# Attention scores of every pass as float32 products in quarters of the array

## The chip, the core and the metric

The kernel runs on one core of a Trainium2 chip. TensorE (PE in the profile) multiplies matrices, VectorE (DVE), ScalarE (ACT) and GpSimd (POOL) do the rest, and SyncE (SP) issues the DMAs, one after another. The metric is the device time of one execution in microseconds; less is better.

## What is computed

Eight batches of eight heads of block-causal attention (576 positions, head size 64, blocks of 64), and behind it a feed-forward layer with a squared ReLU:

```python
scores = scale * np.matmul(q, k.transpose(0, 1, 3, 2))
mask = block_i >= block_j
scores = np.where(mask, scores, -1000000000.0)
scores = scores - np.max(scores, axis=-1, keepdims=True)
attn = np.exp(scores)
attn = attn / (np.sum(attn, axis=-1, keepdims=True) + 1e-09)
out = np.matmul(attn, v)
x = out.transpose(0, 2, 1, 3).reshape(B * S, H * D)      # 4608 x 512
h = x @ w_in                                             # 512 x 2048
g = np.maximum(h, 0.0) ** 2
return g @ w_out                                         # 2048 x 512
```

All arrays are float32. The result is wanted to about float32 precision, so the kernel splits most operands into a high and a low fp16 part and adds two or three fp16 products.

## The kernel before

**Passes.** The attention is cut into 40 passes. A pass takes two heads of one batch (head 0 on partitions 0 to 63, head 1 on 64 to 127) and some of the nine query tiles of 64 rows; query tile j sees key blocks 0 to j. Passes 0 to 7 (batches 0 and 1) take tiles 0 to 2, passes 8 to 15 tiles 3 to 8 of the same batches, and passes 16 to 39 (six batches, four pairs of heads) all nine tiles. The tables G_210, G_86 and so on say which tiles share one score tile `ps` of 1024 columns (two PSUM banks of 512), and at which column each begins. A pass of nine tiles has 45 blocks of 64 queries by 64 keys for each head, in three groups.

**One group** (`softmax`, L431) is a chain: `scores` (L404) on PE into `ps`; row maxima on DVE (L446); exponentials on ACT (L452); the reciprocal of the sums on DVE (L461); the weights into `p_rows`, high part on ACT (L475), low part on DVE (L476); then a transposing DMA into `p_turned` (L480). `values` (L512) multiplies v with `p_turned` into `px`, one accumulation for tiles 0 to 2 and one for tiles 3 to 8. The first 12 passes keep the weights in float32 and turn them on PE (L507) instead.

**Scores, two ways.** Passes 0 to 15 are "native" (NATIVE = 16): q of each head stands alone in a tile `qz` with zeros in the other head's 64 partitions, and a float32 product over all 128 rows of the array writes the head's 64 columns (L411). Passes 16 to 39 use fp16 parts: `front` (L352) takes the largest |q| and |k| (L363), scales, and writes high and low parts into `qs`, `k1` and `k2` (ACT L382, L383; DVE L384, L387, L390, L391); three transposing DMAs (L394 to L396) bring them to `qT` and `kT` with the high part of a head on 64 partitions and its low part on the other 64. Each block of scores is then two fp16 products over 128 rows (z = 0 and 1, L422). In both ways the two heads use the two column halves of the array at once. `front` also makes the fp16 parts of v (L364, L399, L400).

**Loads.** `load(passes[i+2])` stands at the end of pass i. Native passes load `qz` and `kf`, the others `qk32` (tag "qk32", three buffers), and all load v (L347, L349). The same three "qk32" buffers serve the 32 loads of w_out rows: `wa` for the scale, `wb` for the parts (L203 to L206), during passes 8 to 15.

**The feed-forward layer** works on 12 chunks of 384 tokens. `moe_in` (L661) has 16 hidden slices `ph` of 12 fp16 products (L670), then ACT, POOL and DVE form g; `moe_out` (L685) has three outputs `po` of 48 products (L695). These products are laid between the steps of the passes: `pour` takes a set number of them per pass (FILL), `defer` puts `values` and `normalize` a number of such steps later. Before that the weights are split: `weight_parts` (L273) needs DVE, ACT and POOL for each of 16 slices of w_in and 16 of w_out. `first_moe` (chunk 0) has the w_out slices made while it runs.

**Order.** A scheduler with a model of time sets the order of each engine's instructions once, when the program is built; on the chip every engine takes its own in that order. SP, too, issues its DMAs strictly in order, and one that waits holds up those behind it.

## Time and profile before

Three runs took 1155.17 us (median), 1152.74 to 1156.35 us. The profiled execution is one more:

| | |
|---|---|
| profiled execution, own time | 1157.18 us |
| its span, first to last instruction | 1155.4 us |
| mean granted TensorE clock | 0.963 |
| PE busy | 1035.3 us (90%) |
| DVE busy | 763.9 us (66%) |
| ACT busy | 629.6 us (54%) |
| POOL busy | 341.0 us (30%) |
| DMA engines busy, hardware queue | 55.2% |

A row of a group of instructions reads: line, engine, operation, output<-input, shapes, count | busy us, mean ns of one | idle time of the engine before them and what ended it. In a row of the windows each engine has its busy time and, in brackets, its instructions; then come the granted clock (1.00 is full), the share of time in which the DMA engines were busy, and GB/s. A matmul's duration contains its way through the array, so matmuls overlap; the time that one takes from the next is seen in the starts.

### The profile page before, as it was taken

What the parts mean: (1) busy time and instruction counts of PE and PEld (TensorE: products, weight loads), DVE (VectorE), ACT (ScalarE), POOL (GpSimd) and SP (SyncE); (2) the same over time, 40 slices, a digit from 0 to 9 for tenths busy, and PEclk for the clock granted to TensorE, in tenths of its full rate; (3) what the DMA queues carried; (4) which work ended last, traced back from release to release, by engine and by line L of the source; (5) the groups of instructions that cost most, each with busy time, mean ns of one, the idle gap of its engine ahead of it and who ended that gap; (6) DMA issues with size and microseconds to landing.
All of it is one profiled execution on the core that took longest, in us unless ns stands there. A gap on an engine that the chain in (4) does not pass through costs nothing. (4 is left out here: it accounts for less than half of the span.)

```text
span 1155.4 us, 18711 instructions
## 1 busy us (share of the span) xinstructions
PE 1035.3 (90%) x6836; PEld 541.6 (47%) x6836; DVE 763.9 (66%) x1783; ACT 629.6 (54%) x1492; POOL 341.0 (30%) x312
## 2 busy tenths in 40 slices
PE   6679777898989989899997999889889999999998
PEld 4234322354445445445544545445445545555453
DVE  6998789869778978868749857976896613212120
ACT  6586765557468548726737627726865723223140
POOL 2575145124112412422205302520340314312030
PEclk9799998899999999999999999989999999999999
DMA  8555177867687688855954657567848330000000
GB/s 282 194 186 194 56 193 188 198 140 140 144 165 156 114 191 164 155 115 114 186 120 84 141 111 138 119 140 148 170 80 169 48 78 20 10 19 1 28 1 28
DMA packets 337948, 142.25 MB, mean 123 GB/s; under 512 B 309696, under 2 KB 323008, under 8 KB 337856
## 3 DMA queue, kind: packets, MB, share of 16 engines
q1 hardware_dynamic: 337856, 141.06, 55.2%
q8 instruction: 53, 0.87, 0.3%
q14 instruction: 39, 0.32, 0.1%
HBM read 55.31 MB, written 9.44 MB: 56 GB/s over the span
## 5 line engine op out<-in xcount | busy, mean ns | idle before, releaser
L670 PE MATMUL ph<-xt,w1h 128*128 128x384 f16 x1536 | 381.2, 330 | 21.7 <-ACT r L676 10.4
L695 PE MATMUL po<-w2h,g 128*128 128x512 f16 x1152 | 359.7, 386 | 8.5 <-ACT w2h L291 8.5
L679 POOL TENSOR_TENSOR r<-r 128x384 f32<-128x384 f32 x192 | 178.6, 936 | 556.4 <-ACT g L678 520.3
L695 PEld LDWEIGHTS <-g 128*128 128x128 f16 x1728 | 166.3, 99 | 219.4 <-issue 34.1
L670 PE MATMUL ph<-xt,w1l 128*128 128x384 f16 x768 | 253.3, 330 | 0.0
L695 PE MATMUL po<-w2l,g 128*128 128x512 f16 x576 | 222.1, 386 | 4.2 <-POOL w2l L292 4.2
L670 PEld LDWEIGHTS <-w1h 128*128 128x128 f16 x1536 | 145.0, 99 | 129.6 <-issue 34.4
L452 ACT ACTIVATE p<-ps,nmx,es 128x320 f32<-128x320 f32 (+8 forms) x216 | 131.1, 616 | 135.9 <-DVE nmx L449 111.4
L676 ACT ACTIVATE r<-ph 128x384 f32<-128x384 f32 x192 | 93.2, 491 | 160.3 <-PE ph L670 147.9
L680 DVE TENSOR_TENSOR g<-r,g 128x384 f16<-128x384 f32 x184 | 113.7, 623 | 86.3 <-POOL r L679 86.2
L476 DVE SCALAR_TENSOR_TENSOR p_rows<-p,rs,p_rows 128x320 f16<-128x320 f32 (+8 forms) x240 | 143.5, 632 | 18.6 <-ACT p_rows L475 18.3
L475 ACT ACTIVATE p_rows<-p,rs 128x320 f16<-128x320 f32 (+8 forms) x240 | 120.3, 569 | 47.1 <-DVE rs L461 23.1
L446 DVE TENSOR_REDUCE nmx<-ps 128x1 f32<-128x192 f32 (+8 forms) x288 | 124.6, 479 | 23.5 <-PE ps L422 14.8
L678 ACT ACTIVATE g<-r 128x384 f16<-128x384 f32 x192 | 99.4, 525 | 4.0 <-POOL w1l L292 0.8
L670 PEld LDWEIGHTS <-w1l 128*128 128x128 f16 x768 | 75.8, 99 | 51.2 <-issue 2.2
L422 PE MATMUL ps<-kT,qT 128*64 128x64 f16 (+6 forms) x960 | 84.7, 297 | 10.6 <-DMA qT<-qs 5.8
L534 PE MATMUL px<-p_turned,v 128*64 128x384 f16 (+5 forms) x1168 | 79.3, 282 | 14.5 <-DMA p_turned<-p_rows 10.1
L702 DVE TENSOR_SCALAR ob<-po,uv 128x512 f32<-128x512 f32 x36 | 28.9, 805 | 95.7 <-PE po L695 95.7
L534 PEld LDWEIGHTS <-v 128*64 128x64 f16 x1128 | 54.7, 115 | 48.1 <-issue 22.1
L604 POOL TENSOR_TENSOR x<-x,hb 128x768 f32<-128x768 f32 (+1 forms) x16 | 44.6, 2785 | 94.9 <-DVE hb L595 92.8
L422 PEld LDWEIGHTS <-qT 128*64 128x64 f16 x960 | 45.9, 111 | 50.5 <-issue 31.7
L606 POOL TENSOR_TENSOR xt<-x,xt 128x768 f16<-128x768 f32 (+1 forms) x16 | 51.7, 3229 | 30.9 <-DVE xt L605 24.3
(129 smaller groups left out, 965.3 us busy)
## 6 DMA issues: line engine op xcount, KB each, us to landing
qk<-in_qk SPq DMA_DIRECT2D x24, 576.0 KB, 4.5
wa<-in_w_out SPq DMA_DIRECT2D x16, 512.0 KB, 4.3
wb<-in_w_out SPq DMA_DIRECT2D x16, 512.0 KB, 4.4
out<-ob SPq DMA_DIRECT2D x32, 256.0 KB, 2.1
vraw<-in_vm SPq DMA_DIRECT2D x30, 256.0 KB, 3.5
w1raw<-in_w_in SPq DMA_DIRECT2D x8, 512.0 KB, 6.6
kf<-in_qkt SPq DMA_DIRECT2D x8, 288.0 KB, 3.6
w2h<-in_w_in SPq DMA_DIRECT2D x4, 512.0 KB, 10.9
```

The costliest lines, as they stand in the source:

```text
L422: nc.tensor.matmul(ps[hs, o].rearrange("p (n d) -> p n d", d=D), t["qT"][:, j, hs], t["kT"][:, z, c0:c1, hs], start=(z == 0), stop=(z == 1),)
L446: nc.vector.tensor_reduce(nmx[:, i : i + 1], ps[:, off : off + w], axis=AX.X, op=ALU.max, negate=True)
L452: nc.scalar.activation(p32[:, off : off + w], ps[:, off : off + w], AF.Exp, bias=nmx[:, i : i + 1], scale=es, accum_out=sm[:, i : i + 1],)
L475: nc.scalar.activation(hi, p32[:, off : off + w], AF.Copy, scale=rs[:, i : i + 1])
L476: nc.vector.scalar_tensor_tensor(lo, p32[:, off : off + w], rs[:, i : i + 1], hi, op0=ALU.mult, op1=ALU.subtract)
L534: nc.tensor.matmul(px[hs, D * a :].rearrange("p (j d) -> p j d", d=D), lhs, rhs, start=(c == 0 and pi == 0), stop=(c == NCH[g] - 1 and (pi ...
L670: nc.tensor.matmul(ph[:, :CH], w[:, f, P * cc : P * cc + P], xt[:, z, cc, :], start=(i == 0), stop=(i == 11))
L676: nc.scalar.activation(r, ph[:, :CH], AF.Relu, scale=c)
L678: nc.scalar.activation(g[:, 0], r, AF.Square)
L679: nc.gpsimd.tensor_tensor(r, r, r, op=ALU.mult)
L680: (nc.gpsimd if f < G_POOL and ck < G_CK else nc.vector).tensor_tensor(g[:, 1], r, g[:, 0], op=ALU.subtract)
L695: nc.tensor.matmul(po, gs[f][:, z, P * t : P * t + P], w[:, f, :], start=(i == 0), stop=(i == 3 * NF - 1))
```

## The change

All 40 passes get their scores from float32 products, with no fp16 parts of q and k. q and k of a pass are loaded as they are (`qk32`: head h on its 64 partitions), and a product uses only the 64 rows of its head and 64 columns: a quarter of the array. Even query tiles write the columns of their own head, odd query tiles the columns of the other head, so four products can be in four different quarters. The tables are laid out anew so that even tiles lie in the first bank of `ps` and odd tiles in the second. Where an even tile reaches into the second bank (the last block of tile 8, and tile 0 beside it), the product uses all 128 rows with a zero-padded q (`qzs`, two constant tiles, loaded by two small DMAs per pass). `behind` fixes the order of the products of one group among themselves: odd head 0, odd head 1, even head 0, even head 1.

Since odd tiles now hold the heads in swapped halves, `values` has to pick the columns of `p_turned` from alternating halves. `picked` does so: two neighbouring tiles in one product, a left-over tile in one of its own.

```diff
-NATIVE = 16
...
+G_4321 = [(4, 0), (2, 320), (3, 512), (1, 768)]
+G_850 = [(8, 0), (5, 576), (0, 960)]
+G_85 = [(8, 0), (5, 576)]
+G_76 = [(7, 512), (6, 0)]
 G_43 = [(4, 0), (3, 512)]
-G_75 = [(7, 0), (5, 512)]
-G_86 = [(8, 0), (6, 576)]
-G_210 = [(2, 0), (1, 192), (0, 320)]
-G_4230 = [(4, 0), (2, 320), (3, 512), (0, 768)]
-G_751 = [(7, 0), (5, 512), (1, 896)]
+G_210 = [(2, 0), (1, 512), (0, 192)]
...
-G_Y = [(G_86, [], []), (G_75, [3], []), (G_43, [0], [1])]
-G_XY = [(G_4230, [], []), (G_751, [0], [0]), (G_86, [3], [1])]
+G_Y = [(G_85, [], []), (G_76, [3], []), (G_43, [0], [1])]
+G_XY = [(G_4321, [], []), (G_850, [0], [0]), (G_76, [3], [1])]
...
+    qzs = [const.tile([P, 2, 2, D], F32, name=f"qz{i}") for i in range(2)]
+    for t in qzs:
+        for h in range(2):
+            nc.gpsimd.memset(t[D - D * h : P - D * h, h], 0.0)
...
-        for h in range(2):
-            hs, zs = slice(D * h, D * h + D), slice(D - D * h, P - D * h)
-            nc.gpsimd.memset(t[zs, :, h], 0.0)
-            nc.sync.dma_start(t[hs, :, h], qkt[b, hps, hs, 0, :T3].rearrange("c p s -> p c s"))
-        nc.sync.dma_start(t[:, :, 2], qkt[b, hps, :, 1, :T3].rearrange("c p s -> p c s"))
+        for c in range(2):
+            nc.sync.dma_start(t[:, c], qkt[b, hp + c, :, :, :T3])
...
-        if t["native"]:
...
-            t["raw"] = p2.tile([P, 2, S], F32, tag="qk32", name=f"qk32_{u}", bufs=3)
-            nc.sync.dma_start(t["raw"], qk[b - 1, hp])
+        t["qk"] = p2.tile([P, 2, S], F32, tag="qk32", name=f"qk32_{u}", bufs=3)
+        nc.sync.dma_start(t["qk"], qkt[b, hp])
+        t["qz"] = qzs[i % 2]
+        for h in range(2):
+            hs = slice(D * h, D * h + D)
+            nc.sync.dma_start(t["qz"][hs, h], qkt[b, hp, hs, 0].rearrange("p (j d) -> p j d", d=D)[:, 0:9:8, :])
...
-            nc.vector.tensor_reduce(st[:, 0:2], raw, axis=AX.X, op=ALU.max, apply_absolute_value=True)
...
-            nc.scalar.activation(k1[:, :, 0:D], k3, AF.Copy, scale=s[:, 1:2])
-            nc.scalar.activation(qs[:, :, 0:D], q3, AF.Copy, scale=s[:, 0:1])
...
-            nc.vector.tensor_copy(k2[:, :, D:P], k1[:, :, 0:D])
-            nc.vector.tensor_copy(k2[:, :, 0:D], k1[:, :, D:P])
...
-            nc.sync.dma_start_transpose(kT[:, 0], k1.rearrange("p j d -> p (j d)"))
-            nc.sync.dma_start_transpose(qT, qs.rearrange("p j d -> p (j d)"))
-            nc.sync.dma_start_transpose(kT[:, 1], k2.rearrange("p j d -> p (j d)"))
...
+    def scores(t, ps, group):
+        parts = ([], [])
+        for j, off in group:
+            c0 = 0
+            while c0 <= j:
+                c1 = min(j + 1, c0 + 8 - (off // D + c0) % 8)
+                parts[j % 2].append((off + D * c0, j, c0, c1))
+                c0 = c1
+        parts[0].sort()
+        last = None
+        for i in range(max(map(len, parts))):
+            for p in (1, 0):
+                if i >= len(parts[p]):
+                    continue
+                o, j, c0, c1 = parts[p][i]
                 for h in range(2):
+                    hs, rs = slice(D * h, D * h + D), slice(D * (h ^ p), D * (h ^ p) + D)
+                    if o >= 512 and not p:
+                        q, k = t["qz"][:, h, j // 8], t["qk"][:, 1, D * c0 : D * c1]
+                    else:
+                        q, k = t["qk"][hs, 0, D * j : D * j + D], t["qk"][hs, 1, D * c0 : D * c1]
+                    mm = nc.tensor.matmul(ps[rs, o : o + D * (c1 - c0)], q, k, start=True, stop=True)
+                    if last is not None:
+                        behind(mm, last)
+                    last = mm
...
+    def picked(turned, o, n, a, g, h, px):
+        t, e = a, turned.shape[1] + a
+        while t < e:
+            m = (e - t) // 2
+            side = h ^ ((t + 3 * g) & 1)
+            if m:
+                st = n + 1 - 2 * side
+                v = turned[:, t - a : t - a + 2 * m].rearrange("p (m t) b d -> p m (t b) d", t=2)
+                rhs = v[:, :, o + side : o + side + st + 1 : st, :]
+                yield px[:, D * t : D * (t + 2 * m)].rearrange("p (m t d) -> p m t d", t=2, d=D), rhs
+            else:
+                m = 0.5
+                yield px[:, D * t : D * t + D], turned[:, t - a, o + side]
+            t += int(2 * m)
...
+                if not whole and g and c == 2:
+                    a = 0
...
-                native=i < NATIVE, whole=i < WHOLE, last=hp == NHP - 1,
+                whole=i < WHOLE, last=hp == NHP - 1,
```

The host side only arranges the input `qkt` for all eight batches and drops `qk`. Nothing is changed in the feed-forward layer, in FILL and DELAY, or in the softmax but for the scale of the exponential, which is now a constant in all passes.

**The order on PE, first group of pass 24 (batch 4, heads 0 and 1).** `ps` are its scores, `ph` the products of `moe_in` of chunk 4. Before, every block comes as two pairs of fp16 products (each row stands four times):

```order
L670 MATMUL ph_4_6_4949<-xt_4_4141,w1l_97 128x384
L422 LDWEIGHTS qT_4_0_0_4776
L422 MATMUL ps_4_0_0_4_5010<-kT_4_0_0_4777,qT_4_0_0_4776 64x320
...
L422 MATMUL ps_4_0_0_4_5010<-kT_4_0_0_4777,qT_4_0_0_4776 64x192
...
L422 MATMUL ps_4_0_0_4_5010<-kT_4_0_0_4777,qT_4_0_0_4776 64x256
...
L422 MATMUL ps_4_0_0_4_5010<-kT_4_0_0_4777,qT_4_0_0_4776 64x64
L183 LDWEIGHTS ones_bf_78
```

The same group now; where the dots stand, there are the twelve products of a slice `ph`:

```order
L657 MATMUL ph_4_6_4764<-xt_4_4019,w1l_103 128x384
L389 MATMUL ps_4_0_0_4_4827<-qk32_4_0_0_4482 64x256 x2
L657 LDWEIGHTS w1h_102
L657 MATMUL ph_4_7_4789<-xt_4_4019,w1h_102 128x384
...
L389 MATMUL ps_4_0_0_4_4827<-qk32_4_0_0_4482 64x320 x2
L389 MATMUL ps_4_0_0_4_4827<-qk32_4_0_0_4482 64x128 x2
L389 MATMUL ps_4_0_0_4_4827<-qk32_4_0_0_4482 64x192
L657 LDWEIGHTS w1h_102
L657 MATMUL ph_4_8_4808<-xt_4_4019,w1h_102 128x384
...
L389 MATMUL ps_4_0_0_4_4827<-qk32_4_0_0_4482 64x192
```

The group, whole before, now stands in three pieces: the odd tile 3 (256 columns) is alone, and the second head of tile 2 (192) comes twelve products behind the first. Over the 72 groups of passes 16 to 39 there were 118 pieces and 36 unbroken groups before; now there are 111 pieces and 44 unbroken groups, as the one of pass 18, where the rows 64x256, 64x320, 64x128 and 64x192 follow each other.

**The order on SP, the loads of passes 12 and 13 and of w_out.** `qz`, `kf` and `qk32` 1_0 and 1_1 are the q and k of passes 12 and 13, `wb1` the slices of w_out, `vraw` v. Before:

```order
L205 DMA wb1_0_1399<-in_w_out 128x512
L205 DMA wb1_1_1408<-in_w_out 128x512
...
L205 DMA wb1_2_1417<-in_w_out 128x512
L334 DMA qz_1_0_3_1387<-in_qkt 64x384 x2
L335 DMA kf_1_0_3_1388<-in_qkt 128x576
...
L334 DMA qz_1_1_3_1647<-in_qkt 64x384 x2
L335 DMA kf_1_1_3_1648<-in_qkt 128x576
...
L205 DMA wb1_3_1473<-in_w_out 128x512
```

Now:

```order
L327 DMA qk32_1_0_3_1393<-in_qkt 128x1152
L340 DMA vraw1_81<-in_vm 128x2x256
L210 DMA wb1_0_1402<-in_w_out 128x512
...
L210 DMA wb1_1_1411<-in_w_out 128x512
L331 DMA qz0_89<-in_qkt 64x2x64 x2
L210 DMA wb1_2_1420<-in_w_out 128x512
...
L210 DMA wb1_13_1645<-in_w_out 128x512
L342 DMA vraw0_80<-in_vt 64x2x64
L327 DMA qk32_1_1_3_1654<-in_qkt 128x1152
L210 DMA wb1_14_1660<-in_w_out 128x512
```

The q and k of pass 13 moved from before `wb1_3` to behind `wb1_13`, since they now take turns with w_out in the three "qk32" buffers. On PE the scores of pass 13 moved with them: from before the first product of `moe_out` of chunk 0 to behind 78 of its 144.

More of the change, by code (lines that the diff above doesn't have):

```diff
@@ L316, in load_first @@
             passes[NHP * b + hp + c].update(
-                qz=[t[:, c, h] for h in range(2)], kf=t[:, c, 2], chunks=2, v32=o, es=D**-0.5
+                qk=t[:, c], chunks=2, v32=o, es=D**-0.5
             )
@@ L441, in softmax @@
         rs = small.tile([P, n], F32, tag="rs", name=f"rs_{gu}")
-        for j, off in group:
-            scores(t, ps, j, off)
+        scores(t, ps, group)
         for i, (j, off) in enumerate(group):
@@ new lines, in values @@
+                runs = [picked(blocks, o, n, a, g, h, px[D * h : D * h + D]) for h in range(2)]
+                for k, pair in enumerate(zip(*runs)):
+                    for h, (dst, rhs) in enumerate(pair):
+                        nc.tensor.matmul(
+                            dst,
+                            t["v32"][:, h, c, :] if whole else t["v16"][:, zv, h, c, :],
+                            rhs,
+                            start=(c == 0 and pi == 0 and k == 0),
+                            stop=(c == NCH[g] - 1 and (pi == 2 or whole)),
+                            skip_group_check=True,
+                        )
@@ L544, in attention_moe_kernel @@
+        nc.scalar.activation(x, px, AF.Copy, scale=2.0**-A_P if whole else t["xsc"])
     xts = {}
```

117 lines of the change are left out of this document (24 added, 93 removed).

## The prediction

> **What bounds the kernel now.** I read the six stages in the windows first (columns: PE, its weight loads, DVE, ACT, POOL, granted clock, DMA share, GB/s).
>
> ```profile
> 0.00:50.00 50.00, 29.68 (x229) 18.88 (x230) 36.30 (x123) 29.59 (x94) 18.34 (x36) 0.80 0.85 275
> 50.00:100.00 50.00, 38.07 (x239) 20.43 (x239) 49.96 (x98) 37.40 (x82) 37.07 (x34) 1.00 0.51 169
> 100.00:140.00 40.00, 35.73 (x225) 18.32 (x221) 27.82 (x80) 30.06 (x74) 9.95 (x17) 1.00 0.34 103
> 140.00:215.00 75.00, 52.70 (x248) 20.06 (x248) 67.19 (x139) 41.12 (x82) 34.00 (x24) 0.82 0.71 184
> 215.00:910.00 695.00, 639.58 (x4560) 338.02 (x4559) 530.30 (x1252) 426.40 (x1038) 178.85 (x139) 0.97 0.70 139
> 910.00:1155.00 245.00, 239.56 (x1340) 125.87 (x1339) 52.30 (x96) 65.06 (x128) 62.77 (x63) 1.00 0.08 22
> ```
>
> The last 245 us are feed-forward products almost without a gap; so whatever PE finishes earlier up to 910 moves the end by as much. From 215 to 910, the passes with fp16 scores, PE is the bound with 55.4 us of idle time (695 - 639.6) and a clock of 0.97, that is some 21 us of lost clock. From 50 to 100 DVE is the bound (49.96 of 50), from 140 to 215 nearly (67.2 of 75): there PE waits for the weights' parts. Then the waits of PE from 215 to 910 (us in total, times, longest):
>
> ```profile
> PE px L534 <- DMA p_turned<-p_rows: 9.2, 6, 2.5
> PE ph L670 <- DVE ob L702: 7.0, 5, 3.1
> PE ph L670 <- ACT r L676: 6.9, 10, 2.1
> PE nq L589 <- DVE sq L584: 6.5, 4, 2.8
> PE ps L422 <- DMA qT<-qs: 5.8, 4, 3.6
> PE pm L183 <- DVE dg L182: 3.4, 3, 2.0
> PE ps L422 <- ACT p L452: 3.4, 3, 1.5
> PE iv L621 <- DVE ivs L624: 3.0, 2, 2.1
> PE ps L422 <- DMA kT<-k: 1.3, 2, 1.1
> ```
>
> No single wait rules; DVE ends most of them. The lost clock goes with the gaps, as two stretches of 25 us show:
>
> ```profile
> 325.00:350.00 25.00, 21.90 (x182) 12.74 (x181) 20.28 (x47) 18.93 (x46) 6.44 (x6) 0.93 0.78 166
> 575.00:600.00 25.00, 25.00 (x155) 11.82 (x155) 10.36 (x28) 9.84 (x25) 0.00 (x0) 1.00 0.70 140
> ```
>
> With 3.1 us of idle PE the clock is 0.93 on the mean, without any it is full. So a gap costs more than its length.
>
> **The change part by part: the scores on PE.** What a block of 64 by 64 costs both heads is read from starts in the timeline of PE (start, duration, group):
>
> ```profile
> 411.13 0.38 PE L695 MATMUL po<-w2l,g 128*128 128x512 f16 x1
> 411.35 0.38 PE L695 MATMUL po<-w2h,g 128*128 128x512 f16 x1
> 411.66 0.95 PE L422 MATMUL ps<-kT,qT 128*64 128x512 f16 x8
> 412.44 0.48 PE L534 MATMUL px<-p_turned,v 128*64 128x192 f16 x10
> ...
> 22.77 0.88 PE L411 MATMUL ps<-first 128*64 128x192 f32 x12
> 23.48 0.61 PE L534 MATMUL px<-p_turned,vraw 128*64 128x192 f32 x8
> ```
>
> The eight fp16 products are 512 and 384 score columns, two products each, for both heads: 0.78 us until the next group starts, for 14 blocks, 0.056 us a block. The twelve float32 products are two groups of 192, 128 and 64 columns: 0.71 us for 12 blocks, 0.059 us. The column halves work side by side: a `po` product of 512 columns starts 0.22 us before the next, 0.42 ns a column, so the four products of 896 columns would need 1.5 us one after another and took 0.78. So a float32 product costs what two fp16 products cost, as long as only column halves overlap. All that can be won is that now the two row halves work at once as well. No product of before does that. If they don't, nothing is won; if they do fully, only the longer parity counts: 8 blocks in the first group of a pass, 8 and the two zero-padded ones in the second, 8 in the third, 26 in place of 45. But the order breaks groups up. I walked through the 72 groups of passes 16 to 39 as they stand in it, every product starting no earlier than the one before and than its quarter is free, and every piece by itself: 769 block lengths instead of 24 x 26 = 624, and 1173 if the row halves took turns. In time: 24 x 45 x 0.056 = 60.5 us before; now between 769 x 0.059 = 45.4 and 1173 x 0.059 = 69.2 us. I take the lower end, since the column halves do overlap fully in these rows: -15, with +9 as the other bound. The Trainium skill, "TensorE: Matmul & The Clock Gate", Part 3, measures four strips of 32 rows at 3.07 times one strip; by that share, an estimate from its figure, about a quarter of the 24 us between the ends would be missing and the sum 6 us longer. No run here shows it.
>
> Each change of the shape in which the array is used costs a start: 411.35 to 411.66 is 0.31 us where the product alone takes 0.22. Counted through PE's order there are 505 such changes instead of 454: 51 x 0.09 = +5, between 0 and +10.
>
> **The values.** For the short price I take two rows of a window of one `values` (417 to 419.2 us):
>
> ```profile
> L534 PE MATMUL px<-p_turned,v 128*64 128x384 f16 x12 | 1.2, 330 | 0.0
> L534 PE MATMUL px<-p_turned,v 128*64 128x64 f16 x6 | 0.3, 195 | 0.0
> ```
>
> A column costs (330 - 195)/320 = 0.42 ns. In the third key chunk a sixth tile is multiplied: three pairs of 64 columns in 28 passes, 28 x 3 x 0.027 = 2.3 us. The left-over tiles make 228 more pairs with no column more; I give them under 1 us in all, at most 0.03 us each. Together +3, at most +9.
>
> **DVE, ACT and SP.** These groups go, all off PE's path:
>
> ```profile
> L363 DVE TENSOR_REDUCE st<-qk 128x2 f32<-128x1152 f32 x24 | 32.3, 1346 | 21.5 <-DMA qk<-in_qk 21.3
> L387 DVE SCALAR_TENSOR_TENSOR qs<-qk,s,qs 128x576 f16<-128x576 f32 x24 | 24.7, 1028 | 0.0
> L384 DVE SCALAR_TENSOR_TENSOR k<-qk,s,k 128x576 f16<-128x576 f32 x24 | 19.5, 810 | 5.4 <-ACT k L382 5.4
> L390 DVE COPY k<-k 128x576 f16<-128x576 f16 x24 | 10.8, 452 | 0.0
> L391 DVE COPY k<-k 128x576 f16<-128x576 f16 x24 | 9.4, 393 | 0.0
> L382 ACT ACTIVATE k<-qk,s 128x576 f16<-128x576 f32 x24 | 18.6, 773 | 16.7 <-DVE s L191 16.7
> L383 ACT ACTIVATE qs<-qk,s 128x576 f16<-128x576 f32 x24 | 18.4, 766 | 0.0
> L452 ACT ACTIVATE p<-ps,nmx,es 128x576 f32<-128x576 f32 x24 | 20.0, 832 | 57.9 <-DVE nmx L449 42.4 <-PE nq L589 12.3 <-DVE mx L180 2.9
> L452 ACT ACTIVATE p<-ps,nmx 128x576 f32<-128x576 f32 x8 | 5.9, 739 | 3.1 <-DVE nmx L449 2.1 <-DVE p_rows L476 1.0
> L395 SPq DMA_TRANSPOSE qT<-qs x24: 1276/1325/2372, 236.3 to 884.0; - x24
> L480 SPq DMA_TRANSPOSE p_turned<-p_rows x56: 4404/4621/7538, 157.9 to 942.1; - x56
> ```
>
> DVE loses 32.3 + 24.7 + 19.5 + 10.8 + 9.4 = 96.7 of its 530 us and 21 us of waiting in which what stood behind waited too. ACT loses 37.0 us, and the exponential with a constant scale is 93 ns shorter (832 against 739) in 216 calls, another 20. SP loses 72 transposes of 1.3 us, which held up the transposes of `p_turned` (4.6 us of SP each) and the loads of v; it gains two small loads a pass. This work is hidden behind PE now, so it counts only by PE's idle time. Of the 55.4 us: the waits for `qT` and `kT` go (7); of those for `p_turned` half (-5); of those for DVE (7.0 + 6.5 + 3.4 + 3.0 in the rows and 5 in smaller ones, 25 in all) a third, since DVE loses a fifth of its work and its stalls for q and k (-8); of those for ACT (some 13) a quarter (-3). That is -23, and the lost clock falls in the same proportion, 21 x 23/55 = -9. Together -32; at the ends 0, if new gaps open in their place, and -60. What is late next at such places is `p_turned`, whose transpose itself stays.
>
> **The first 215 us.** Passes 8 to 15 come down from 39 to 22 blocks, 1 us of PE each, but only from 100 to 140, some three passes, is PE the bound: -3. Against it, q and k of these passes now take the buffers of w_out. Before:
>
> ```profile
> L205 SPq DMA_DIRECT2D wa<-in_w_out x16: 327/328/535, 42.7 to 98.5; - x16
> wa<-in_w_out SPq DMA_DIRECT2D x16, 512.0 KB, 4.3
> L245 DVE TENSOR_REDUCE stw<-wa 128x1 f32<-128x512 f32 x16 | 10.7, 675 | 0.1
> PE po L695 <- ACT w2h L291: 8.5, 7, 2.2
> ```
>
> By the waits in the order, seven of the first eight `wa` follow each other in one buffer, each after 0.33 + 4.3 + 0.68 = 5.3 us, and the last eight share two. 7 x 5.3 + 4 x 5.3 = 58 us from 42.7 puts the last reduction at 101 at best; before, the last one was issued at 98.5 and landed at 103. But before, three buffers could have done the sixteen in 28 us and took 56, since other work held them up; if those 28 us come on top now as well, the last is 26 late. I take +6, between 0 and +26. From 140 to 215 PE waits for w_out's parts (last row) and passes 13 to 15 filled the time; now five groups of passes 14 and 15 (27 blocks, 1.6 us), one `values` (66 blocks of 64 columns, 1.8 us) and some ten starts (0.9) come later, when PE has no room. +5, between 0 and +20.
>
> **Sum.** -15 + 5 + 3 - 32 - 3 + 6 + 5 = -31 us. The profiled execution took 1157.2, so 1126.2; the median of the runs lies 2.0 under it: **1124 us**.
>
> **The rivals.** (a) The row halves take turns: 69.2 instead of 45.4 us, +24: 1148. For it: no row shows them together. Against it: the column halves overlap without loss, and the quarters are fed by no more rows than they. (b) PE's gaps don't close, because each gap is ended by something else a moment later (`p_turned`, `ob`): +32, 1156, no change. For it: the waits are spread over nine kinds; against it: DVE stands in most of them and gets a fifth less to do. (c) The buffers of w_out: `wa` 26 late, `wb1_1` and `wb1_2` loaded only behind the scores of passes 11 and 12 (one load, +5), and all of passes 13 to 15 out of the stage (3 x 4): +43 in place of +11, 1156. For it: DVE takes its work in order, and from 50 to 100 it has no time to give away; against it: with three buffers the loads were no limit before. (d) Slower: the two row halves can't write one bank of PSUM at a time. In the new layout the two heads of one parity always do (odd tiles the second bank, even tiles the first). Walked through the order with that rule, in which head 1 waits for head 0 and everything behind it waits as well, it is 1642 block lengths, 96.9 us, +51: 1175. It decides from 31 us on, that is where a pass costs 1.3 us more than forecast here. In these rows only column halves ever write one bank together, which says nothing on it. The Trainium skill states it, "TensorEngine Tiling (Array Packing)", section "Restrictions and Gotchas": different row tiles can't access the same bank at the same time. The trace has no row for or against; that the two heads write different partitions speaks for its not applying.
>
> **How the numbers follow.** Forecast, 1100 to 1140: 0.53. Better than that: 0.08. (a) 0.12, (b) 0.12, (c) 0.06, (d) 0.09. The range from 1100 to 1157 leaves out the better case and (d) with some of (b), about 0.2. A difference of 0.3%, 3.5 us, is about what a measurement of this kernel can tell from none. Faster by more: the forecast, the better case, (a), and a quarter of (b) and (c), 0.53 + 0.08 + 0.12 + 0.05 = 0.78. Within it: half of (b) and (c), 0.09. Slower: (d) and the last quarter of (b) and (c), 0.13.
>
> **What would show it.** Products starting in fours almost at once, and a whole first group taking about 0.5 us (8 x 0.059), show the row halves together; second pairs that start when the first end show (a); head 1 starting when head 0 ends shows (d). PE's idle time in the stage of passes 16 to 39 should fall from 55 to about 32 us and its clock rise to 0.98; DVE should be busy some 100 us less in all, ACT some 57. The end of chunk 0's `moe_out` should come at about 220 us. If scores take 45 us and the idle time stays at 55, (b) was right.

## The result, and the profile after

The changed kernel took 1195.8 us (median of 4 runs, 1193.8 to 1197.1), the kernel before 1155.8: 1.035 times as long, 95% interval 1.0325 to 1.0375. The forecast of 1124 had the wrong sign, and 1196 lies outside its range. The profiled execution has a span of 1192.0 us at a mean clock of 0.954. Its stages, in the columns of the windows of before:

```profile
0.00:50.00 50.00, 30.69 (x261) 19.78 (x261) 36.11 (x128) 30.44 (x94) 15.26 (x26) 0.75 0.76 261
50.00:100.00 50.00, 37.85 (x221) 18.84 (x220) 47.67 (x84) 36.79 (x82) 39.47 (x32) 0.84 0.31 97
100.00:140.00 40.00, 29.41 (x201) 16.02 (x201) 23.34 (x59) 21.89 (x55) 6.84 (x9) 0.89 0.64 197
140.00:215.00 75.00, 47.80 (x261) 20.37 (x254) 58.51 (x131) 36.29 (x67) 30.68 (x23) 0.83 0.52 145
215.00:910.00 695.00, 644.87 (x4679) 318.67 (x4679) 438.93 (x1093) 372.59 (x968) 163.44 (x135) 0.98 0.55 115
910.00:1192.00 282.00, 273.16 (x1599) 142.81 (x1597) 74.02 (x148) 85.22 (x181) 67.71 (x69) 0.99 0.12 27
```

From 215 to 910 DVE and ACT did lose their work (530 to 439 us, 426 to 373), and the clock rose from 0.97 to 0.98. PE, though, is busier than before (640 to 645) in the same 695 us, and at 910 there is more left to do: the last stage is 282 us, not 245.

Fixed windows mix stages that have shifted. So I mark the stages by the feed-forward products, which are the same 4032 in both kernels, and sum for each tile PE's time from one start to the next, with the idle time that the trace shows set apart (us). "To the 480th" is the time until the 480th product starts (about when the passes with all nine tiles set in); "steady" runs from there to the 2980th, with nearly all of passes 16 to 39. The last column has the scores of all these 24 passes, wherever they stand, and in brackets how much of them was done before the 480th product:

| | to the 480th | steady | scores | values | idle | rest of steady | all scores of passes 16 to 39 |
|---|---|---|---|---|---|---|---|
| before | 263.4 | 689.9 | 74.5 | 58.8 | 54.7 | 501.9 | 77.3 (2.8) |
| after | 279.5 | 711.1 | 101.9 | 63.3 | 48.4 | 497.5 | 105.0 (3.1) |

From the 2980th product to the start of the last one both need the same 197.3 us. So of 37 us in the trace 16 arise before the 480th product and 21 in the steady stage: scores +27.4, values +4.5, idle -6.3, the rest -4.4.

The scores cost more, not less. Two groups of them in PE's timeline of the changed kernel:

```profile
561.02 1.08 PE L389 MATMUL ps<-qk 64*64 64x512 f32 x8
562.03 0.27 PE L182 MATMUL pm<-ident,st 128*1 128x128 f32 x1
562.23 1.09 PE L389 MATMUL ps<-qk 64*64 64x256 f32 x16
563.25 0.50 PE L657 MATMUL ph<-xt,w1h 128*128 128x384 f16 x2
```

The first is tiles 7 and 6, one product for each tile and head: four products, and the row says x8. The second is tiles 4, 3, 2, 1, eight products, and the row says x16. So a float32 product is two records. The same holds in the kernel before, in the group on which the prediction's price rests:

```profile
L411 PE MATMUL ps<-first x96: 219/314/580, 5.2 to 23.4; 128*64 128x192 f32 x32, 128*64 128x128 f32 x32, 128*64 128x64 f32 x32
```

Eight passes with three tiles and two heads are 48 products, and there are 96 records. The "x12" at 22.77 in the prediction's rows was one group of six products, not two groups: 0.71 us for 6 blocks, 0.118 us a block and not 0.059.

What the prediction had open came out well. In the group at 561.02 the first records of its four products, one in each quarter, start at 561.021, .028, .034 and .041, and the next product behind the group 1.01 us after the first. It holds 15 blocks; one after another at 0.118 they would take 1.77, the longer parity alone 0.94. All four quarters work at once.

PE's and DVE's waits from 215 to 910:

```profile
PE pm L188 <- DVE dg L187: 14.4, 8, 4.0
PE iv L608 <- ACT x L528: 7.1, 3, 3.2
PE px L520 <- DMA p_turned<-p_rows: 6.9, 6, 1.8
```

```profile
DVE st L353 <- DMA vraw<-in_vt: 62.8, 22, 6.2
```

The waits for `qT` and `kT` are gone, but PE now waits for `dg`, 14.4 us instead of 3.4, and DVE stands 62.8 us waiting for v. How the two hang together shows at 342 to 352 us in the timelines of SP, DVE and PE:

```profile
336.67 5.04 SPq L442 DMA_TRANSPOSE p_turned<-p_rows  x1
341.81 0.53 SPq L327 DMA_DIRECT2D qk<-in_qkt  x1
342.44 0.60 SPq L340 DMA_DIRECT2D vraw<-in_vm  x1
343.08 0.60 SPq L342 DMA_DIRECT2D vraw<-in_vt  x1
```

```profile
341.57 0.17 DVE L423 RECIPROCAL rs<-sm 128x2 f32<-128x2 f32 x1
347.68 0.82 DVE L353 TENSOR_REDUCE st<-vraw 128x1 f32<-128x640 f32 x1 [5.94 <-DMA vraw<-in_vt]
348.42 1.34 DVE L438 SCALAR_TENSOR_TENSOR p_rows<-p,rs,p_rows 128x512 f16<-128x512 f32 x2
349.67 1.28 DVE L408 TENSOR_REDUCE nmx<-ps 128x1 f32<-128x320 f32 x4
351.77 0.20 DVE L187 TENSOR_SCALAR dg<-ident,mx 1x1 bf16<-1x1 f32 x1
```

```profile
347.62 0.45 PE L520 MATMUL px<-p_turned,v 128*64 128x128 f16 x11
352.02 0.16 PE L188 MATMUL pm<-dg,ones_bf 1*128 1x1 bf16 x1 [3.96 <-DVE dg L187]
```

DVE comes to the largest |v| (`st`) of a later pass at 341.74, when SP has only just ended a transpose (336.67 to 341.71) and hasn't yet issued the load of that v (342.44 and 343.08). It stands for 5.9 us; `p_rows`, the row maxima and `dg`, whose operands are there, stand behind it; and PE in turn waits 4 us for `dg`. In DVE's order `st` follows four rows behind the instruction that frees v's buffer, a whole pass before the program writes it, as here for pass 26:

```
719 L361 SCALAR_TENSOR_TENSOR v16_4_0_0_4596<-vraw0_80,s_4_0_0_4592,v16_4_0_0_4596 128x640
...
723 L353 TENSOR_REDUCE st_4_2_0_5238<-vraw0_80 128x1
724 L438 SCALAR_TENSOR_TENSOR p_rows_84<-p32_3_3_0_8_4677,rs_3_3_0_8_4680,p_rows_84 128x576
```

The kernel before has this too (34.6 us of waits for v and 20.0 for q and k from 300 to 900 us).

### The profile page after: what moved, and what is told of

Read it like the earlier page. It is cut to its first block, busy times and chain, and to the rows that moved or that the text cites. A ratio compares the mean times of both kernels' runs of the same rounds, so it can differ in the third digit from the quotient of the medians.

```text
span 1192.0 us, 19186 instructions
## 1 busy us (share of the span) xinstructions
PE 1063.8 (89%) x7212; PEld 536.5 (45%) x7212; DVE 678.6 (57%) x1639; ACT 583.2 (49%) x1444; POOL 323.4 (27%) x292
## 5 line engine op out<-in xcount | busy, mean ns | idle before, releaser
L666 POOL TENSOR_TENSOR r<-r 128x384 f32<-128x384 f32 x192 | 172.7, 902 | 626.8 <-ACT g L665 596.3
L414 ACT ACTIVATE p<-ps,nmx 128x192 f32<-128x192 f32 (+8 forms) x288 | 148.4, 524 | 222.2 <-DVE nmx L411 197.6
L438 DVE SCALAR_TENSOR_TENSOR p_rows<-p,rs,p_rows 128x576 f16<-128x576 f32 (+8 forms) x240 | 147.4, 650 | 44.6 <-ACT p_rows L437 44.3
L667 DVE TENSOR_TENSOR g<-r,g 128x384 f16<-128x384 f32 x184 | 107.0, 583 | 100.4 <-POOL r L666 100.4
L437 ACT ACTIVATE p_rows<-p,rs 128x576 f16<-128x576 f32 (+8 forms) x240 | 120.5, 565 | 51.1 <-DVE rs L423 25.7
L389 PE MATMUL ps<-qk 64*64 64x384 f32 (+4 forms) x960 | 130.2, 508 | 11.2 <-ACT p L414 5.9
L657 PEld LDWEIGHTS <-w1l 128*128 128x128 f16 x768 | 76.1, 99 | 59.3 <-issue 5.8
L520 PE MATMUL px<-p_turned,v 128*64 128x64 f16 (+4 forms) x1496 | 81.8, 259 | 13.7 <-DMA p_turned<-p_rows 9.3
L591 POOL TENSOR_TENSOR x<-x,hb 128x768 f32<-128x768 f32 (+1 forms) x16 | 45.2, 2822 | 98.7 <-DVE hb L582 86.1
L422 DVE TENSOR_SCALAR sm<-sm 128x2 f32<-128x2 f32 (+2 forms) x104 | 32.1, 309 | 69.7 <-ACT p L414 69.4
L353 DVE TENSOR_REDUCE st<-vraw 128x1 f32<-128x640 f32 x28 | 23.0, 820 | 67.4 <-DMA vraw<-in_vt 67.3
```

The costliest lines, as they stand in the source:

```text
L389: mm = nc.tensor.matmul(ps[rs, o : o + D * (c1 - c0)], q, k, start=True, stop=True)
L414: nc.scalar.activation(p32[:, off : off + w], ps[:, off : off + w], AF.Exp, bias=nmx[:, i : i + 1], scale=es, accum_out=sm[:, i : i + 1],)
L437: nc.scalar.activation(hi, p32[:, off : off + w], AF.Copy, scale=rs[:, i : i + 1])
L438: nc.vector.scalar_tensor_tensor(lo, p32[:, off : off + w], rs[:, i : i + 1], hi, op0=ALU.mult, op1=ALU.subtract)
L520: nc.tensor.matmul(dst, t["v32"][:, h, c, :] if whole else t["v16"][:, zv, h, c, :], rhs, start=(c == 0 and pi == 0 and k == 0), stop=(c = ...
L657: nc.tensor.matmul(ph[:, :CH], w[:, f, P * cc : P * cc + P], xt[:, z, cc, :], start=(i == 0), stop=(i == 11))
```

## The experiments

My theory after the result, the **price theory**: a float32 product costs twice what I took, and that is the loss. Its rival, the **order theory**: the place of instructions in the engines' queues, set by the scheduler anew for each program, costs the time (gaps, broken groups, the buffers of w_out). Medians in us, the 95% interval of the ratio to the kernel before in the same series (there it took 1155.9 to 1157.3), and the stages as above:

| | time | ratio | to the 480th | steady | scores | values | idle | all scores of passes 16 to 39 |
|---|---|---|---|---|---|---|---|---|
| e1 top halves | 1108.4 | 0.957 to 0.961 | 266.5 | 638.9 | 30.8 | 62.1 | 47.4 | 32.5 (1.8) |
| e2 full rows | 1164.6 | 1.006 to 1.012 | 262.8 | 699.0 | 138.8 | 59.3 | 11.2 | 142.8 (3.9) |
| e3 early only | 1180.0 | 1.019 to 1.024 | 267.8 | 708.8 | 76.2 | 60.4 | 65.9 | 76.2 (0.0) |
| e4 late only | 1177.1 | 1.017 to 1.022 | 264.7 | 709.0 | 101.7 | 62.6 | 49.9 | 106.1 (4.4) |
| e5 own buffers | 1185.8 | 1.019 to 1.027 | 276.1 | 706.3 | 95.9 | 63.6 | 45.8 | 105.3 (9.4) |
| e6 held st | 1155.2 | 0.996 to 1.001 | 280.5 | 672.0 | 86.1 | 60.6 | 29.5 | 90.7 (4.6) |
| e7 four qz | 1190.2 | 1.026 to 1.031 | 277.5 | 708.0 | 102.8 | 62.5 | 43.1 | 105.5 (2.7) |
| e8 before, held | 1134.2 | 0.977 to 0.982 | 266.0 | 661.1 | 67.3 | 53.7 | 44.7 | 70.7 (3.4) |
| e9 early, held | 1148.4 | 0.992 to 0.996 | 279.8 | 660.7 | 67.9 | 52.8 | 41.3 | 69.7 (1.8) |
| e10 late, held | 1134.2 | 0.978 to 0.985 | 268.9 | 662.7 | 82.7 | 60.6 | 27.0 | 90.6 (7.8) |
| e11 held, own buffers | 1142.4 | 0.985 to 0.993 | 276.6 | 662.6 | 83.3 | 60.9 | 26.0 | 93.0 (9.6) |
| e12 full rows, held | 1170.7 | 1.010 to 1.018 | 282.8 | 684.6 | 127.7 | 55.9 | 8.8 | 144.0 (16.4) |
| e13 before, v held | 1181.8 | 1.021 to 1.025 | 266.9 | 709.2 | 72.1 | 58.9 | 74.9 | 75.5 (3.4) |

**e1, the upper halves of q and k.**

```diff
+                    q, k = (a.bitcast(BF16).rearrange("p (n t) -> p n t", t=2)[:, :, 1] for a in (q, k))
                     mm = nc.tensor.matmul(ps[rs, o : o + D * (c1 - c0)], q, k, start=True, stop=True)
```

> The changed kernel with one edit: every score product reads only the upper 16 bits of q and k (as bfloat16, every second half-word of the same float32 tiles). The lower halves of q and k are left out of the scores. Order, groups, loads and values are as in the changed kernel. Price theory: each float32 product stands in the trace as two records and takes about four times the array time of a 16-bit product (0.107 to 0.118 us a block against 0.027), so the scores, 145 us of PE's start-to-start time in the changed kernel, fall to some 40 to 50, and each product has one record in place of two; the kernel takes 1110 to 1135 us. Order theory (the time goes into gaps, broken groups and the shared buffers, and a float32 product costs no more than two 16-bit ones): at most 45 us fewer on PE and the gaps stay, 1150 to 1175 us.

1108.4 us, 87 under the changed kernel, a little more than the price theory allowed. Its groups of products, and one group of tiles 4, 3, 2, 1 in the timeline:

```profile
L390 PE MATMUL ps<-qk 64*64 64x384 bf16 (+3 forms) x480 | 42.8, 355 | 14.8 <-ACT p L415 11.9 <-DMA qk<-in_qkt 2.8
L390 PE MATMUL ps<-qk,qz 128*64 128x64 bf16 x112 | 8.2, 211 | 0.0
L390 PE MATMUL ps<-first 64*64 64x128 bf16 (+2 forms) x48 | 3.2, 290 | 7.5 <-DMA first<-in_qkt 5.6 <-ACT p L415 2.0
```

```profile
301.62 0.42 PE L390 MATMUL ps<-qk 64*64 64x256 bf16 x8
301.97 0.39 PE L683 MATMUL po<-w2h,g 128*128 128x512 f16 x1
```

The records are 640, one for each product, where the changed kernel has 1280 (960 + 224 + 96). The group takes 0.35 us to the next start; in float32 (at 562.23) it took 1.02. The scores of the steady stage fall by 71 us. That is the price of the second half of q's and k's bits. The idle time, however, stays at 47.4: the gaps are a matter of their own.

**e2, native scores over all rows.**

```diff
-NATIVE = 16
+NATIVE = 40
-    qkt = np.ascontiguousarray(both[:, :2].transpose(1, 2, 3, 6, 0, 4, 5)).reshape(2, NHP, P, 2, S)
+    qkt = np.ascontiguousarray(both.transpose(1, 2, 3, 6, 0, 4, 5)).reshape(B, NHP, P, 2, S)
```

> The kernel before with one edit: its native float32 scores, zero-padded q over all 128 rows with only the column halves at once, for all 40 passes; old tables, old values, no quarters. Price theory with quarters that overlap: passes 16 to 39 take 24 x 45 x 0.118 = 127 us of PE for scores in place of some 75 in the kernel before and 102 in the changed one; less some 6 us of closed gaps and without the 4.5 us of the new values, 1195 to 1220 us, and scores longer than the changed kernel's by about 25 us. If row halves take turns and the quarters bring nothing: scores no longer than the changed kernel's 102 us in these passes, and the time under 1190.

Scores 138.8 us, 37 over the changed kernel, where the price theory had 127 and 25: the quarters do bring something, and the price is of the right size. But the time, 1164.6, is far under the 1195 to 1220 expected, and under the changed kernel. One line of the windows says why:

```profile
300.00:900.00 600.00, 591.43 (x3909) 303.14 (x3909) 375.38 (x949) 319.48 (x837) 161.90 (x156) 1.00 0.50 108
```

PE is idle for 8.6 of 600 us and the clock is full. PE's gaps do close here, 54.7 to 11.2 us; the changed kernel took the same work from DVE and kept 48.4. Price alone doesn't explain the result. Nor is it shown that DVE's lighter work closed them: PE has 64 us more of scores here, in which DVE can catch up, and DVE still waits 39.6 us for loads of v from 300 to 900 us, which PE hardly feels.

**e3 and e4, the change in one half of the passes.** Both are the two kernels put together by a switch on the number of the pass (in both the zero-padded tiles of q come from a pool):

```diff
-                native=i < NATIVE, whole=i < WHOLE, last=hp == NHP - 1,
+                native=i < NATIVE, quart=i in QUART, whole=i < WHOLE, last=hp == NHP - 1,
...
+        if t["quart"]:
+            scores_q(t, ps, group)
+        for j, off in () if t["quart"] else group:
```

> The change for passes 0 to 15 alone; passes 16 to 39 keep their fp16 parts, old tables and old values (the two zero-padded tiles of q come from a pool and are cleared in each pass). Price theory: the changed kernel is 16 us late at its 480th feed-forward product and loses some 21 more behind it; here only the first part stays, 1160 to 1172 us. If the early passes displace work of later ones and so carry most of the loss: 1180 or more. If nothing of the early part matters to the end: 1153 to 1158.

> The change for passes 16 to 39 alone; passes 0 to 15 as in the kernel before, so that q and k of passes 8 to 15 stay out of the buffers of w_out. Price theory: the steady stage costs 27 us more of scores and 4.5 more of values, less some 6 of closed gaps, 1175 to 1185 us. If the loss lies in the early passes and the shared buffers: 1150 to 1162. With the prediction's prices: 1116 to 1130.

e4 came out as expected (1177): scores +27.2, values +3.8, idle -4.8 against before. e3 did not. It is only 4 us late at the 480th product, and then loses 19 more with the very instructions of the kernel before: idle 65.9 instead of 54.7, and 4.4 us more for what is neither scores nor values. The scores of passes 16 to 39 cost no more than before (76.2 and 77.3). So hardly any of it is work pushed into this stage; what differs there, I took it, is the order, and e9 below bears that out.

**e5, buffers of their own for w_out.**

```diff
-        raw = p2.tile([P, 512], I64, tag="qk32", name=name, bufs=3)
+        raw = p2.tile([P, 512], I64, tag="w32", name=name, bufs=3)
```

(and `first` takes the same buffers, for room.)

> The changed kernel, with the loads of w_out's rows (wa, wb) in three buffers of their own, so that q and k of passes 8 to 15 no longer stand in their ring. The changed kernel is 16 us behind the kernel before at its 480th feed-forward product. Ring theory: most of these come from the ring; the lag there falls to 6 or less and the time to 1182 to 1188 us. Order theory (the lag comes from where the scheduler puts passes 8 to 15 and w_out's parts): the lag stays at 12 to 18 and the time at 1190 to 1200.

10 us faster, as the ring theory had it, but with a lag of 12.7 us at the 480th product (expected 6 or less). The part of the stage up to product 192 recovers (17.3 late falls to 2.9), and the next one gives most of that back. In part that is other work: by the 480th product 9.4 us of the scores of passes 16 to 39 are done, where the changed kernel had done 3.1. So its lower scores in the steady stage aren't cheaper ones either; all 24 passes cost the same (105.3 and 105.0).

**e6, `st` held back.** The reduction that waits for v is put behind the row maxima of the present pass's first group, in DVE's order; no wait is added by it, but the scheduler makes the whole order anew around it:

```diff
-        nc.vector.tensor_scalar(nmx, nmx, es, None, op0=ALU.mult)
+        seen["nmx"] = nc.vector.tensor_scalar(nmx, nmx, es, None, op0=ALU.mult)
...
-        nc.vector.tensor_reduce(st, v32, axis=AX.XYZ, op=ALU.max, apply_absolute_value=True)
+        i = nc.vector.tensor_reduce(st, v32, axis=AX.XYZ, op=ALU.max, apply_absolute_value=True)
+        behind(i, seen["nmx"])
```

> The changed kernel with one more constraint on the order of DVE: the largest |v| of the next pass (st) is taken only behind the row maxima of the present pass's first group, where the program writes it, in place of right behind the release of its buffer, where the scheduler had moved it and DVE waited 60 us in all for v to land. Order theory: the 48 us of PE's idle time in the steady stage come from such waits of DVE, with the rows that PE needs queued behind; DVE's waits for v fall under 15 us, PE's idle time to 15 to 25, its waits for dg from 14 to under 4, and the time to 1160 to 1175. If PE's gaps come from the change itself (shorter scores, other groups), whatever DVE waits for: idle stays at 42 or more and the time at 1188 to 1200.

1155.2 us: 41 us gained by one such constraint per pass, more than expected. DVE's longest sums of waits from 300 to 900 us:

```profile
DVE sm L425 <- ACT p L417: 52.1, 43, 2.0
DVE ob L692 <- PE po L685: 35.8, 13, 9.6
DVE p_rows L441 <- ACT p_rows L440: 35.0, 45, 5.1
```

and PE's wait for `dg` in the same time:

```profile
PE pm L188 <- DVE dg L187: 2.4, 4, 0.8
```

No wait of `st` is left. PE's idle time falls from 48.4 to 29.5 (expected 15 to 25). The scores fall too, from 101.9 to 86.1 (all 24 passes from 105.0 to 90.7), which I had not expected. Between 300 and 915 us they stand in 80 unbroken stretches instead of 93. A group that isn't broken up takes 1.03 (4, 3, 2, 1), 1.40 (8, 5, 0) and 1.0 (7, 6), 24 x 3.43 = 82 us for all; so some 23 of the changed kernel's 105 us are its broken groups. The gain is thus not DVE's waits alone: 19 us of it are idle time and 14 are groups that PE's new order leaves whole.

**e7, four zero-padded tiles of q.**

```diff
-    qzs = [const.tile([P, 2, 2, D], F32, name=f"qz{i}") for i in range(2)]
+    qzs = [const.tile([P, 2, 2, D], F32, name=f"qz{i}") for i in range(4)]
...
-        t["qz"] = qzs[i % 2]
+        t["qz"] = qzs[i % 4]
```

> The changed kernel with four zero-padded tiles of q in place of two, so that SP need not wait for the scores of the pass two back (19 waits, 71 us in all) before it loads them, with v's load queued behind. If that queue is what brings v late: DVE's 60 us of waits for v fall under 40, PE's idle time in the steady stage from 48 to under 38, 1175 to 1188 us. If SP's waits are slack, or v is late because its own buffer comes free late: 1192 to 1198.

1190.2, between the two; DVE's wait for v doesn't move (59.4 us from 270 to 960, 59.9 in the changed kernel). But neither does SP's wait, which the edit was to take away; from 270 to 960 us, in the changed kernel and here:

```profile
SPq L331 <- PE ps L389: 70.7, 19, 11.8
SPq L331 <- PE ps L389: 76.1, 17, 12.2
```

So whether that wait brings v late stays open.

**e8, the kernel before with the same hold** on the largest |q|, |k| and |v|:

```diff
-            nc.vector.tensor_reduce(st[:, 0:2], raw, axis=AX.X, op=ALU.max, apply_absolute_value=True)
+            i = nc.vector.tensor_reduce(st[:, 0:2], raw, axis=AX.X, op=ALU.max, apply_absolute_value=True)
+            behind(i, seen["nmx"])
-        nc.vector.tensor_reduce(st[:, 2:3], v32, axis=AX.XYZ, op=ALU.max, apply_absolute_value=True)
+        i = nc.vector.tensor_reduce(st[:, 2:3], v32, axis=AX.XYZ, op=ALU.max, apply_absolute_value=True)
+        behind(i, seen["nmx"])
```

> The kernel before with the same constraint: the largest |q|, |k| and |v| of the next pass only behind the row maxima of the present pass's first group; DVE waited 55 us for these loads from 270 us on. Order theory: DVE's waits for them fall under 15 us and PE's idle time in the steady stage (55 us) to 30 to 40: 1132 to 1145 us. Rival: the fp16 parts of q and k then come too late for the next pass's scores, and PE waits for qT and kT instead: 1155 to 1175.

1134.2 us, 0.979 of the kernel before: faster than either kernel. Idle falls only from 54.7 to 44.7 (expected 30 to 40), with the scores, values and the rest shorter by 19 together at a clock of 0.99; 1.8 us of the values have moved behind the steady stage. What PE waits for most from 300 to 900 us:

```profile
PE ph L674 <- ACT r L680: 15.6, 10, 2.5
PE ps L424 <- DMA qT<-qs: 8.2, 7, 2.9
PE pm L183 <- DVE dg L182: 5.3, 3, 2.2
PE iv L625 <- DVE m L185: 4.3, 3, 2.9
PE ps L424 <- DMA kT<-k: 3.6, 5, 1.1
```

**e9 to e12, the parts of the change under the hold.** e9 is e3, e10 is e4 and e12 is e2, each with the edit of e8; e11 is e5 with the edit of e6. In all four the line that matters is the same:

```diff
+        behind(i, seen["nmx"])
```

> The change for passes 0 to 15 alone, with the constraint on the largest values (st behind the row maxima of the present pass's first group) in all passes. Without it this kernel lost 19 us behind its 480th feed-forward product, where its instructions are those of the kernel before. Order theory: those 19 us were DVE's waits for loads; they go, and the kernel comes to 1134 to 1146 us, 0 to 12 over the kernel before with the same constraint (1134). If the early passes push real work into the later ones: 1152 or more.

> The change for passes 16 to 39 alone, with the same constraint. Price theory: under one rule of order the quarters still cost PE 12 to 25 us more than the fp16 parts in these passes, and some of it comes back in gaps: 1140 to 1152 us, slower than the kernel before with the constraint (1134). If float32 quarters were as cheap as the prediction had them: under 1125.

> The changed kernel with the constraint and with w_out's loads in buffers of their own. If the two losses are separate, their gains add: 1155 less some 10, 1142 to 1149 us. If the constraint already took what the buffers gave: 1152 to 1158.

> The kernel before with native float32 scores over all rows in every pass, with the same constraint. There PE has only 11 us of idle time in the steady stage, so closing gaps has nothing to give: 1155 to 1166 us (1164.6 without). If the constraint gains by something else than DVE's waits, such as less broken groups of scores: 1140 to 1153.

e9: 1148.4. Its steady stage is that of e8 to 0.4 us (660.7 and 661.1), so e3's 19 us were order; it is 14 us late at the 480th product, and this lag is all its loss, which makes the time 2 us more than expected. e10: 1134.2, better than the price theory's 1140. The quarters do cost PE 15.4 us of scores and 6.9 of values against e8 in the steady stage, but the idle time gives 17.7 back (44.7 to 27.0); over the whole runs, so that it doesn't matter where the work stands, it is 21.3 and 5.6 against 21.9. Under one rule of order the change to passes 16 to 39 is neutral. e11: 1142.4, the gains of e5 and e6 add. e12: 1170.7, no gain, as the order theory had it for a kernel without gaps, though 5 us over its range. Its steady stage is 14 us shorter and its way to the 480th product 20 us longer, mostly because work has moved: 16.4 us of the later passes' scores are done before the 480th product, 3.9 in e2. All 24 passes cost as much as in e2 (144.0 and 142.8), so the hold made no scores cheaper here, and the 39.6 us of DVE's waits for v that went with it had cost nothing that shows in the time.

**e13, only |v| held in the kernel before.** Against e8:

```diff
-            i = nc.vector.tensor_reduce(st[:, 0:2], raw, axis=AX.X, op=ALU.max, apply_absolute_value=True)
-            behind(i, seen["nmx"])
+            nc.vector.tensor_reduce(st[:, 0:2], raw, axis=AX.X, op=ALU.max, apply_absolute_value=True)
```

> The kernel before with the constraint on the largest |v| alone (pm and the scale still need all three values, so the fp16 parts of q and k wait for it too); the largest |q| and |k| may be taken as early as before. If it was the late start of q's and k's parts that made PE wait for qT and kT: PE's waits for them fall from 11.8 to under 6 us and the time to 1122 to 1130, so that the fp16 scores of passes 16 to 39 are still the better ones by 5 us or more. If these waits come from the transposing DMAs or from the common scale: 1130 to 1140, as with both held, and the change to these passes is neutral under this rule. If DVE then waits for q and k again: 1140 to 1150.

1181.8, none of the three: 48 us slower than e8 with the same work. The reduction of q and k now stands where that of v stood, from 300 to 900 us:

```profile
DVE st L363 <- DMA qk<-in_qk: 71.4, 18, 7.6
```

```profile
PE pm L183 <- DVE dg L182: 21.5, 9, 4.7
```

So DVE's waits for loads of a later pass are 0 in e8, 55 in the kernel before and 71 here, PE's idle time is 44.7, 54.7 and 74.9, and the time 1134, 1156 and 1182. e3 and e2 warn against reading this as a law: 57.5 us of such waits with 65.9 of idle time, and 39.6 with 11.2. Whether e8's waits for `qT` and `kT` could be had away, and the fp16 scores then be the better ones by that much, stays open.

## Why the prediction was wrong

**The scores (-15, bounds -15 to +9; measured +27.4).** The step that failed: "The twelve float32 products are two groups of 192, 128 and 64 columns: 0.71 us for 12 blocks, 0.059 us." They were twelve records of six products. With 0.118 the same step gives 769 x 0.118 = 90.7 against 60.5, +30. The quarters overlap, as forecast, and the walk through the order was good: an unbroken pass takes 3.43 us for 26 block lengths, 0.132 a block, and 769 of them make 101.5; all 24 passes took 105.0. Both prices a block were somewhat low, since the scores of the kernel before took 77.3, not 60.5, but that leaves the difference as it is (+27.7). Being 42 us, this step is the largest part of the miss. The sum would have been +14 with nothing else changed: the sign turns on this one count. It could have been seen beforehand: 96 records for 48 products in the row above. A float32 product thus costs 0.118 us a block against 0.028 for one fp16 product of it (half of 0.056). The Trainium skill, "FP8 and Floating Point Precision", section "TensorE Precision Notes", has true FP32 take four passes through the array; the trace agrees, with 4.2 times the price. In quarters, with the starts in it, float32 is 3.2 times the 16-bit products (105.0 and 32.5 us for all 24 passes, e1).

**Idle time and clock (-32).** The gaps can close: 54.7 to 11.2 with the clock at 1.00 in e2, and 17.7 us less in e10 than in e8. But in both PE has more scores to do as well (64 and 15 us), so that DVE's lighter work is the cause is argued, not shown; in e1, with the same lighter work and cheaper scores, idle stays at 47.4. In the changed kernel only 6.3 of the 23 us came. The rest of the stage is 4.4 us shorter, which is what the clock and the starts (-9 and +5) make together, but no run parts the two. The step that failed is what is late next: not `p_turned` but v, in DVE's own queue, by an order that the scheduler made with the change. That is rival (b) in its effect. Its reason was named too generally: PE's largest wait, for `dg`, stood behind one head, `st`, and the constraint on it, with the order that came of it, gave 41 us (e6).

**Values (+3, at most +9; measured +4.5).** As forecast: over the whole runs it is +5.7, and +5.6 under the hold (e10 against e8).

**The first 215 us (-3 + 6 + 5 = +8; measured +16 to the 480th product).** Within the bounds given, but made up otherwise. The shared buffers cost 10 to 13 us in all (e5 against the changed kernel, e11 against e6), near the +6 and +5 that the prediction gave for what they do. From the 336th to the 480th product the scores cost 8.4 us instead of 2.8: the displaced passes, as forecast. What failed is the -3, for the PE time that these passes save. Up to the 480th product the scores do take 12.0 us less, but PE's idle time is 16.7 us longer, and the same 480 feed-forward products take 8.2 us more. The sum had no term for this. The clock from 50 to 100 us is 0.84 where it was 1.00, and 0.89 from 100 to 140, with the same PE busy in the first of these stretches (37.85 and 38.07 us). All eight kernels with the change to passes 0 to 15 have 0.80 to 0.86 from 50 to 100, the seven without it 0.97 to 1.00. What differs in PE's waits from 50 to 140 us is their length, first before, then now:

```profile
PE pt L507 <- DVE p_turned L509: 3.7, 3, 2.1
```

```profile
PE pt L469 <- DVE p_turned L471: 11.3, 4, 4.5
PE ps L389 <- DMA qk<-in_qkt: 4.0, 1, 4.0
```

The wait for q and k is gone in e5, with buffers of their own; why DVE's copies of the turned weights come later is open. So is how much of the 16 us is order: e3 has 4, e9 14, with the same early passes.

**What it said would show it.** A group of eight block lengths took 1.01 us, not "about 0.5"; DVE is busy 85 us less in all (763.9 to 678.6), near the 100; ACT 46 (629.6 to 583.2), near the 57; chunk 0's `moe_out` ends at 235 us, not 220. The kernel before has it at 229, so the 220 didn't go with the sum's own +8.

**The rivals.** (a) and (d) are refuted by starts 7 ns apart and by the 1.01 us of the group: the two heads of tile 7 use different row halves and write one bank. So here the rule of the Trainium skill, "TensorEngine Tiling (Array Packing)", "Restrictions and Gotchas", doesn't hold as it is worded, and the measurement decides. (c) had the right place, but 10 to 13 us instead of 43.

**The ledger.** Forecast -31, measured +37 in the trace, 68 us apart: scores 42, idle 17, values 1.5, the early passes 8. How the 40 us of the medians come about: under the hold the change costs 1155.2 - 1134.2 = 21, of which the early passes alone are 14, the late ones alone 0, and 7 come with both. The other 19 I call order: the hold takes 41 from the changed kernel and 22 from the kernel before. Since a scheduler sets the whole order anew for every edit, the size of this last share belongs to these two programs.

## What to carry to other kernels

Before a price is taken from a row with a count, count that operation in the code: a product may be several records. An engine that works strictly in order and meets an instruction whose load has just been issued makes everybody behind it wait; look for the short, early instruction at the head of such waits and put it later, before rebuilding what is slow, and measure it: with only one of two such reductions put later the other took its place, and the kernel was 48 us slower (e13 against e8). Judge a change under the same rule of order in both kernels: here that turned the 21 us that the change to passes 16 to 39 costs by itself (e4) into none (e10 against e8).

## What the runs showed of the hardware

- A float32 product is two records and costs 0.118 us for 64 columns in both heads' column halves; the same group of eight quarter products took 1.02 us in float32 and 0.35 in 16 bits (e1).
- Four quarters of 64 by 64 run at once, also when two row halves write one PSUM bank: 15 blocks in 1.01 us, where the longer parity alone would be 0.94. The quarter of the gain that I had taken as missing in the estimate from the Trainium skill, "TensorE: Matmul & The Clock Gate", Part 3, isn't: 0.07 of the 0.83 us between 1.77 and 0.94 is, some 8%.
- With 8.6 us of gaps in 600 PE's clock was 1.00 (e2); with 8% of idle time (the kernel before, 215 to 910 us) it was 0.97. The share of idle time alone doesn't set it: from 50 to 100 us the kernel before had 12 us of it, in waits of up to 2.1 us, at a clock of 1.00; the changed kernel as much, in waits of up to 4.5 us, at 0.84.
